# Numbers fetched two steps behind their list, logits in the ring of banks, measuring products at the head of a step

## The chip, the cores and the metric

The kernel runs on one core of a Trainium2 chip. The metric is the device time of one execution in microseconds. The kernel before took 1575.07 us in the median of three runs.

## The reference

A long convolution with a gate, and a mixture of experts with one expert for each token behind it. Shapes: B=4, S=11456, D=128, E=8 experts with F=1024 hidden values.

```python
h_filt = (maximum(pos_emb @ w1, 0) @ w2) * exp(-0.01 * pos)[:, None]
u = x * v
y = irfft(rfft(u, n=2*S) * rfft(h_filt, n=2*S))[:, :S, :]
x = (x * y).reshape(B * S, D)                # the rows of the second half

do_compute = x @ w_skip > 0                  # rows that go through an expert
e_idx = argmax(x[do_compute] @ w_gate)       # its one expert
gate_w = softmax(...)[e_idx]
out = x.copy()
out[do_compute] += gate_w * (maximum(x @ w1[e], 0) @ w2[e])
```

## The kernel before

The program has four parts, one behind the other on each engine: `first_phase` (filter and first transform), `freq_phase` (products in the frequency domain), `out_phase` (last transform, routing and the first expert work) and `late_slots` (the rest of the expert work). The change touches only `out_phase` and the generator `early_slots` that runs inside it.

`out_phase` makes the rows in NCH = 32 chunks of 128 x 12 rows. A chunk `ch` passes through a row of small jobs: `product` (matmuls of the last transform on TensorE, and a multiplication by x on VectorE, L1112, into the tile `xm`), `turned` (transposes), `score` and `score2` (the nine logits of each row, computed turned and then turned back), `choose` (the expert of each row, VectorE), `exp` and `gate`, `count`, `total` and `full` (how many rows each expert gets), `measure` and `ranks` (small matmuls), `measured` and `route` (VectorE), `spread` (one-hot tables on VectorE, in the first FRONT = 7 chunks partly on GpSimd), `collect`, `lay`, `laid`, `write` (the list of row numbers, written to HBM by an indirect DMA of GpSimd, L615).

The order is written by hand. Time is cut into steps; three steps belong to a chunk, so chunk `ch` begins at step `first(ch)` = 0, 4, 7, 10, 13, and on by threes. A table gives each job a lag in steps behind `first(ch)` and an order within its step (a number; jobs of all chunks that fall into one step are sorted by it). So three kinds of step follow each other: those with lags 0, 3, 6, 9, 12 (called step A below), with lags 1, 4, 7, 10 (step B) and with lags 2, 5, 8, 11 (step C). Every instruction is issued in exactly the order that results; an engine never passes an instruction that waits.

Expert work is handed out between the jobs. `next(work)` stands at order 0.5 of each step, and because `PACE` is 1.24 it is called once more at the end of about every fourth step. It issues a piece of `early_slots`: 'up' matmuls (L730 to L732) or 'down' matmuls (L813) of a group of 256 or 512 rows, or the preparation of the next group.

Before an expert can work on rows, these things happen one after the other: the list of a chunk is written (L615, GpSimd's queue); at a few chunks (`KNOWN`) a `table` is computed in five stages that alternate between VectorE and TensorE (L557 to L606; its final stage reads the products of L585 to L587 from PSUM at L590 to L594); `name`, at order 7.5 of each step, fetches the numbers of at most two groups from the list into SBUF (L625, SyncE's queue); one step later the group has its name, and `ex.more()` gathers its rows by two indirect DMAs (L667, GpSimd's queue); and `prepare` splits the weights and transposes the rows (L719). For the first group `prepare` waits a fixed number of steps for the gathered rows.

PSUM: `opy` is a ring of three banks called `wide`, used by `product`, `turned` and `score`. `opl` holds three fixed banks: bank 0 is shared by counting, measuring, ranks and the tables, bank 1 belongs to the down products, bank 2 holds the turned logits `lgp` beside `places` and `lies` (the results of `collect` and `lay`). The dependencies go by bank: who writes a bank waits for all that still read from it.

SyncE's queue carries, in this order of the program, the loads of x (`ox`, L1078) and of the transformed data (`zt`, L1087), the stores of finished chunks (L1116), and the fetches of numbers (L625).

## Time and profile before

| | |
|---|---|
| median of 3 runs | 1575.07 us (1573.11 to 1578.29) |
| the profiled execution, its own time | 1581.42 us |
| its span, first to last instruction | 1579.6 us |
| mean granted clock of TensorE | 0.973 of full speed |
| TensorE busy | 1484.2 us (94% of the span) |
| VectorE busy | 1130.7 us (72%) |
| GpSimd busy | 1080.7 us (68%) |
| ScalarE busy | 755.1 us (48%) |

The profiled execution is 6.35 us longer than the median; 1.8 us of its time lie around the span. Times below are those of this one execution, counted from the span's start. "Idle before" is the time in which an engine had nothing to run, and the arrow names the instruction whose end released it. PEclk is the clock that TensorE was granted: 1.00 is 2.4 GHz and 0.50 is 1.2 GHz.

### The profile page before, as it was taken

The page shows a single profiled execution, that of the slowest core. Times are in us where ns is not written, and L with a number is a line of the kernel's source. Part 1 is how long each engine was busy: PE and PEld are TensorE (multiplying, and loading weights), DVE is VectorE, ACT ScalarE, POOL GpSimd, SP SyncE. Part 2 cuts the span into 40 slices and gives each one's busy share as a digit, 9 for nine tenths or more (in the row PEclk, how much of TensorE's full clock was granted, in tenths as well). Part 3 has the DMA queues.
Part 4 walks back from the last instruction along what each step waited for, and adds up shares of the span by engine and source line. Part 5 has one row for each costly group of instructions (what it writes and reads, how often), then busy time and mean ns, then how long its engine had stood idle before and what let it go on. Part 6 is the DMA issues. An engine that isn't in the chain of part 4 may idle for free. (4 is left out here: it accounts for less than half of the span.)

```text
span 1579.6 us, 24184 instructions
## 1 busy us (share of the span) xinstructions
PE 1484.2 (94%) x7360; PEld 931.2 (59%) x7360; DVE 1130.7 (72%) x2323; ACT 755.1 (48%) x1509; POOL 1080.7 (68%) x832
## 2 busy tenths in 40 slices
PE   8976999999999999998759999999989999999998
PEld 3542444444444444443437767777777888888888
DVE  2324877888788889996757877777766777777774
ACT  5542555544545444442224554444535555555554
POOL 2102988888888878882157566875777888888756
PEclk9996999999999999999789999999989999999999
DMA  9998999999999978978968888988521111111100
GB/s 322 332 337 316 382 372 375 359 331 331 314 353 330 311 237 271 351 202 286 352 193 259 252 276 263 283 282 249 174 63 35 46 46 45 46 46 43 43 25 29
DMA packets 200376, 361.82 MB, mean 229 GB/s; under 512 B 64492, under 2 KB 140762, under 8 KB 200206
## 3 DMA queue, kind: packets, MB, share of 16 engines
q1 hardware_dynamic: 181078, 317.04, 59.5%
q0 software_dynamic: 16448, 38.88, 8.5%
q10 hardware_dynamic: 2720, 4.34, 0.9%
q8 instruction: 59, 0.97, 0.3%
q14 instruction: 71, 0.58, 0.1%
HBM read 216.77 MB, written 145.42 MB: 229 GB/s over the span
## 5 line engine op out<-in xcount | busy, mean ns | idle before, releaser
L412 PE MATMUL ps<-y,c 128*128 128x512 f32 x720 | 331.3, 597 | 0.3
L480 POOL TENSOR_TENSOR y<-y,p 128x2048 f32<-128x2048 f32 x59 | 267.8, 4538 | 70.0 <-DVE p L401 70.0
L736 POOL DMA_INDIRECT out<-o,ids x182 | 199.3, 1095 | 116.3 <-DVE o L743 78.6
L412 PEld LDWEIGHTS ps<-y,c 128*128 128x128 f32 x720 | 133.4, 190 | 173.0 <-issue 156.5
L667 POOL DMA_INDIRECT xt<-out,ids x182 | 192.8, 1059 | 58.4 <-issue 29.1
L401 DVE TENSOR_TENSOR p<-xp,g 128x1024 f32<-128x1024 f32 x240 | 217.4, 948 | 0.0
L401 DVE TENSOR_TENSOR y<-xp,g 128x1536 f32<-128x1536 f32 x120 | 210.9, 1757 | 4.0
L852 DVE SCALAR_TENSOR_TENSOR hh<-hp,hh 128x1024 fp32r<-128x1024 f32 x122 | 148.7, 1219 | 88.9 <-ACT hh L851 75.5
L413 ACT COPY z<-ps 128x512 f32<-128x512 f32 x180 | 105.6, 586 | 178.3 <-PE ps L412 158.6
L851 ACT ACTIVATE hh<-hp 128x1024 fp32r<-128x1024 f32 x122 | 126.4, 1036 | 92.1 <-issue 70.4
L481 POOL TENSOR_TENSOR y<-y,p 128x1024 f32<-128x1024 f32 x59 | 139.1, 2357 | 4.6
L640 POOL MEMSET idle<- 128x512 f16 x231 | 126.3, 547 | 0.3
L381 PE MATMUL xp<-x,wf 128*128 128x480 f32 x256 | 117.4, 583 | 9.1 <-DMA x<-x1f 5.9
L210 PE MATMUL ps<-wf,c 60*120 60x384 f32 x512 | 112.6, 536 | 11.6 <-DVE wf L193 11.6
L212 ACT COPY wf<-ps 120x384 f32<-120x384 f32 x256 | 105.6, 493 | 27.0 <-PE ps L210 23.8
L813 PE MATMUL bank<-wd,h 128*128 128x128 f32 x896 | 114.8, 286 | 0.0
L193 POOL TENSOR_TENSOR wf<-wf 124x768 f32<-124x768 f32 x45 | 82.0, 1822 | 47.5 <-DVE g L394 47.4
L813 PEld LDWEIGHTS bank<-wd,h 128*128 128x128 f32 x896 | 108.0, 198 | 0.3
L730 PE MATMUL hp<-hl,ws 128*128 128x512 f32 (+1 forms) x256 | 103.2, 403 | 2.6 <-issue 1.5
L393 DVE TENSOR_TENSOR g<-xp,g 128x128 f32<-128x128 f32 x120 | 34.8, 290 | 97.2 <-ACT g L386 97.1
L384 ACT COPY g<-xp 64x192 f32<-64x192 f32 x120 | 38.0, 317 | 137.4 <-PE xp L381 94.7
L707 DVE TENSOR_TENSOR ws<-wf,ws 128x1024 fp32r<-128x1024 f32 x82 | 99.9, 1218 | 5.0 <-issue 3.2
(199 smaller groups left out, 2851.3 us busy)
## 6 DMA issues: line engine op xcount, KB each, us to landing
wf<-xv SPq DMA_DIRECT2D x64, 768.0 KB
x1d<-wf SPq DMA_DIRECT2D x64, 720.0 KB
x<-x1d SPq DMA_DIRECT2D x60, 768.0 KB
zt<-zd SPq DMA_DIRECT2D x60, 768.0 KB
zd<-z SPq DMA_DIRECT2D x110, 384.0 KB
out<-xm SPq DMA_DIRECT2D x96, 258.0 KB
ox<-xo SPq DMA_DIRECT2D x96, 256.0 KB
x1f<-fx POOLq DMA_DIRECT2D x16, 720.0 KB
```

The lines of the kernel that those rows point to most:

```text
L210: nc.tensor.matmul(ps[p], self.c1[rows], u[rows, q * RUN:(q + 1) * RUN], start=True, stop=True)
L381: nc.tensor.matmul(xp[:, k, 0:(NS + NB) * DH], c2(n % PER * KS + j * KH + k), x1[:, j * KH + k], start=True, stop=True)
L401: nc.vector.tensor_tensor(o[:, :, :, j * KH:(j + 1) * KH].rearrange("p s a k b d -> p (s a) k b d"), x[:, None].broadcast_to([128, m, KH, ...
L412: nc.tensor.matmul(zps, c3[:, a, :], y[:, blk, a], start=(a == 0), stop=(a == 1))
L480: nc.gpsimd.tensor_tensor(y[:, 1:], y[:, 1:], p1, ALU.add)
L481: nc.gpsimd.tensor_tensor(y[:, 2:], y[:, 2:], p2, ALU.add)
L640: self.nc.gpsimd.memset(self.idle, 0.0)
L667: ins = nc.gpsimd.indirect_dma_start(out=xt[:, j], out_offset=None, in_=self.rows[0:have], in_offset=bass.IndirectOffsetOnAxis(ap=ids[:, j ...
L736: ins = nc.gpsimd.indirect_dma_start(out=self.rows, out_offset=bass.IndirectOffsetOnAxis(ap=ids[:, j:j + 1], axis=0), in_=o, in_offset=Non ...
L813: nc.tensor.matmul(bank[:, j * D:(j + 1) * D], h[f][:, j * 128:(j + 1) * 128], wd[s][:, f * D:(f + 1) * D], start=(f == 0), stop=(f == F / ...
L851: nc.scalar.activation(h[:, 0], hp, AF.Relu)
L852: nc.vector.scalar_tensor_tensor(h[:, 1], hp, 0.0, h[:, 0].bitcast(F32), ALU.max, ALU.subtract)
```

## The change

Six things are done. `STORE` goes from 7 to 6: each store is issued one step sooner. `prepare` waits three steps instead of two for the rows of the first group. `lgp`, the logits turned back, are no longer in bank 2 but in a bank of the ring `wide`, and `score2` moves behind `turned`, from order 2 to 4.2 of its step. `name` fetches the numbers of a list only if the list was written two steps ago, not one. `measure` and `ranks` move from the end of step C (lag 8) to the head of the following step A (lag 9), and with them `measured` and `routed`, which were already there, move behind the first call of `tabled` at order -1.5, so that a table begins and ends one step later. `spread` moves from the head of step C (lag 11) to the middle of the step B before it (lag 10), and the second half of the load of `zt` from lag 1 to the end of lag 0.

```diff
-STORE = 7
+STORE = 6
...
-                for _ in range(4 if s else 2):
+                for _ in range(4 if s else 3):
                     yield
...
-        lgp = bank[2][:, 0:NB * 128].rearrange("p (s t) -> p s t", s=NB)
-        places, lies = bank[2][0:PQ, 384:384 + PL], bank[2][0:PQ, 384 + PL:385 + PL]
+        places, lies = bank[2][0:PQ, 0:PL], bank[2][0:PQ, PL:PL + 1]
...
         def score2(ch):
             lt = chunks.pop(ch)
+            lgp = wide()[:, 0:NB * 128].rearrange("p (s t) -> p s t", s=NB)
...
-                if b not in ex.tabled or written.get(ch, at[0]) >= at[0]:
+                if b not in ex.tabled or written.get(ch, at[0]) >= at[0] - 1:
                     return
...
-                    (0, 0, produced), (1, 0.1, lambda ch: load_z(ch + ZB, 1)), (1, 4, turned),
-                    (3, -0.1, score), (4, 2, score2), (5, 3, choose), (6, 1, exp), (6, 4.5, count), (6, 6, counted), (6, 6, gate), (7, 4.4, total),
-                    (8, -2.5, full), (8, 4.4, measure), (8, 4.5, ranks),
-                    (9, -2.3, measured), (9, -2, routed), (11, -2.4, spread), (12, 0.2, collect), (12, 0.3, lay), (12, 2.5, laid), (12, 2.6, write)):
+                    (0, 0, produced), (0, 8.9, lambda ch: load_z(ch + ZB, 1)), (1, 4, turned),
+                    (3, -0.1, score), (4, 4.2, score2), (5, 3, choose), (6, 1, exp), (6, 4.5, count), (6, 6, counted), (6, 6, gate), (7, 4.4, total),
+                    (8, -2.5, full), (9, -0.4, measure), (9, -0.35, ranks),
+                    (9, -0.3, measured), (9, -0.2, routed), (10, 3, spread), (12, 0.2, collect), (12, 0.3, lay), (12, 2.5, laid), (12, 2.6, write)):
```

Lines 1055 to 1137 of the kernel before have numbers one lower in the changed kernel.

**The first group on TensorE.** The rows L719 are the transposes of the first group's gathered rows; L571 to L587 are the table of the chunk with index 4; L1178 counts the experts of a chunk. Before, TensorE came to L719 in the step B of chunk 7, right behind the first products of that table:

```order
L1178 LDWEIGHTS oh
L1178 MATMUL bank_4478<-ones,oh 96x1
L571 LDWEIGHTS shift
L571 MATMUL bank_4478<-tnt,shift 8x1
L572 LDWEIGHTS shift
L572 MATMUL bank_4478<-done,shift 8x1
L719 MATMUL mh<-ident,xt_4442 128x128 x2
L1140 MATMUL bank_4480<-ident,lt 128x128 x3
L1124 MATMUL wide<-ident,xm 128x128 x12
```

Now L719 stands in the step B of chunk 8, three steps later; the rest of the table, and the measuring, logits, products and collecting of a whole chunk (L1198 to L1213, here from the last rows of the collecting on), are in front of it, and `score2` (L1140) is behind the transposes of `turned` (L1123, before L1124):

```order
L1250 MATMUL bank_4480<-hl,hq 53x32
L1213 MATMUL bank_4480<-ge_4481 53x1
L1178 LDWEIGHTS oh
L1178 MATMUL bank_4478<-ones,oh 96x1
L719 MATMUL mh<-ident,xt_4442 128x128 x2
L1123 MATMUL wide<-ident,xm 128x128 x12
L1140 MATMUL wide<-ident,lt 128x128 x3
```

So the work of three steps moved from behind the first group's transposes to ahead of them.

**The first fetch on SyncE.** L625 is the fetch of a group's numbers (with L623 and a register operation for its address), here of the first two groups. Before, the loads of x and `zt` for the next chunk stood behind it and behind a second pair of fetches:

```order
L1087 DMA zt<-zd 128x4x384
L623 TENSOR_LOAD addr
L623 ISA x2
L625 REGISTER_ALU
L625 DMA ids<-lists 128x2
```

Now one more store stands ahead of the first pair, and loads of the next chunk come right behind it, ahead of the second pair:

```order
L1115 DMA out<-xm 128x516 x2
L623 TENSOR_LOAD addr
L623 ISA x2
L625 REGISTER_ALU
L625 DMA ids<-lists 128x2
L623 TENSOR_LOAD addr
L623 ISA x2
L625 REGISTER_ALU
L625 DMA ids<-lists 128x2
L1115 DMA out<-xm 128x516
L1075 DMA c_5265<-c 128x256
L1077 DMA ox<-xo 128x512 x3
```

The first pair of fetches moved one step towards the end of the program.

**A table and the measuring product on TensorE.** L585 to L587 are the last products of a table (that of the chunk with index 8, with three entries), L1198 is the measuring product; both use bank 0. Before, a piece of expert work (L813, 'down') stood between them:

```order
L586 MATMUL bank_4478<-tpast,tstep 1x3
L587 LDWEIGHTS done
L587 MATMUL bank_4478<-first,done 1x3
L813 MATMUL bank_4479<-wd,h 128x128 x8
L1198 LDWEIGHTS sums
L1198 MATMUL bank_4478<-ct,sums 128x2
```

Now nothing stands between them:

```order
L586 MATMUL bank_4478<-tpast,tstep 1x3
L587 LDWEIGHTS done
L587 MATMUL bank_4478<-first,done 1x3
L1198 LDWEIGHTS sums
L1198 MATMUL bank_4478<-ct,sums 128x2
```

On VectorE the final stage of the same table (L590 to L594) stood behind `full` and `spread` (L1242, L1244). Now it stands behind `choose` (L1149 to L1159), and `measure` waits for its last row:

```order
L582 CAST tph<-tpast 8x3
L1149 TENSOR_REDUCE mx<-lg 128x12
L1151 TENSOR_TENSOR df<-lg,mx 128x96
L1153 SCALAR_TENSOR_TENSOR wt<-df,rev 128x96
L1155 TENSOR_REDUCE mw<-wt 128x12
L1157 SCALAR_TENSOR_TENSOR me<-lg,mw 128x12
L1159 TENSOR_TENSOR oh<-rev,me 128x96
L590 SCALAR_TENSOR_TENSOR trow<-iota,bank_4478 1x3
L593 TENSOR_SCALAR addr<-trow 1x3
L594 TENSOR_SCALAR tab<-bank_4478 1x3
```

The table's last stage moved one step on, to the head of the step in which the measuring product is now.

## Rows read from the trace of the kernel before

**Rows 1.** Busy time by stretch: bounds in us, then for each engine busy us and (instructions), then the granted clock, the DMA share and GB/s. `out_phase` begins at 731.5 us. The first stretch ends with the first group's transposes; in the second, expert work runs beside the jobs of the chunks; the third holds the end of `out_phase`; the last is `late_slots` without its end.

```profile
801.00:816.00 15.00, 1.19 (x5) 0.90 (x6) 4.38 (x16) 1.40 (x3) 9.85 (x11) 0.62 0.62 188
830.00:1140.00 310.00, 297.15 (x2435) 220.18 (x2434) 234.31 (x891) 146.98 (x298) 213.92 (x250) 1.00 0.82 258
1140.00:1196.00 56.00, 50.56 (x353) 42.81 (x352) 32.36 (x135) 19.73 (x33) 43.14 (x51) 0.91 0.26 57
1196.00:1540.00 344.00, 341.41 (x1617) 281.81 (x1618) 256.46 (x371) 200.71 (x234) 265.46 (x276) 1.00 0.16 42
```

**Rows 2.** Timeline of TensorE around the first group's transposes: start us, busy us, the instruction, [idle before it and what ended that].

```profile
800.79 0.16 PE L571 MATMUL bank<-tnt,shift 8*8 8x1 f16 x1 [0.99 <-DVE tnt L565]
...
810.63 0.48 PE L719 MATMUL mh<-ident,xt 128*128 128x128 f32 x1 [9.65 <-DMA xt<-out,ids]
815.29 0.47 PE L719 MATMUL mh<-ident,xt 128*128 128x128 f32 x1 [4.19 <-DMA xt<-out,ids]
...
816.20 2.52 PE L1124 MATMUL wide<-ident,xm 128*128 128x128 f32 x12
...
818.82 0.39 PE L730 MATMUL mh<-hl,ws 128*128 128x256 f32 x1
```

**Rows 3.** Timeline of SyncE's queue at the same place (issues of DMAs; the waits for semaphores are not rows of it).

```profile
793.93 0.42 SPq L1087 DMA_DIRECT2D zt<-zd  x1
802.56 1.46 SPq L625 DMA_DIRECT2D ids<-lists  x2
...
807.72 1.34 SPq L1078 DMA_DIRECT2D ox<-xo  x3
```

**Rows 4.** Timeline of GpSimd at the same place.

```profile
793.18 1.59 POOL L615 DMA_INDIRECT lists<-pl,lies  x1 [7.37 <-DVE sm L1170]
...
805.28 2.12 POOL L667 DMA_INDIRECT xt<-out,ids  x1 [7.72 <-DMA ids<-lists]
...
808.12 1.02 POOL L667 DMA_INDIRECT xt<-out,ids  x1 [0.17 <-issue]
```

**Rows 5.** Busy time by stretch, columns as in rows 1: one chunk without expert work, first as TensorE passes it and then as VectorE does, and the 3 us behind the wait of rows 2.

```profile
792.90:800.80 7.90, 6.24 (x57) 3.69 (x58) 5.94 (x28) 2.58 (x6) 2.96 (x3) 1.00 0.91 288
794.80:803.70 8.90, 4.55 (x42) 1.96 (x41) 8.21 (x36) 2.73 (x6) 1.34 (x2) 1.00 0.66 207
815.00:818.00 3.00, 2.71 (x13) 2.71 (x14) 0.47 (x2) 1.21 (x3) 2.67 (x4) 0.50 1.06 358
```

**Rows 6.** Timeline of VectorE between 777 and 803 us.

```profile
777.12 1.89 DVE L1112 TENSOR_TENSOR xm<-wide,ox 128x512 f32<-128x512 f32 x3 [0.96 <-DMA out<-xm]
...
794.85 0.15 DVE L1191 TENSOR_SCALAR nt<-bank 96x1 int32<-96x1 f32 x1 [1.35 <-PE bank L1186]
...
795.30 0.81 DVE L1242 TENSOR_TENSOR hq<-grid,tf 128x636 f16<-128x636 f16 x1
796.03 0.55 DVE L1242 TENSOR_TENSOR hl<-grid,tf 128x384 f16<-128x384 f16 x1
...
802.87 0.18 DVE L1257 SCALAR_TENSOR_TENSOR pl<-bank,no 53x32 int32<-53x32 f32 x1
```

**Rows 7.** Waits of TensorE between 830 and 1140 us: who waited <- for whom: us in total, times, longest us.

```profile
PE bank L1198 <- DVE tdn L599: 4.5, 3, 1.8
PE bank L1250 <- POOL hl L1244: 2.9, 1, 2.9
...
PE bank L1140 <- DVE pl L1257: 1.4, 2, 1.1
PE bank L1198 <- DVE tab L594: 1.3, 1, 1.3
```

**Rows 8.** Timelines at the table of the chunk with index 8, TensorE first, then VectorE.

```profile
873.24 0.16 PE L587 MATMUL bank<-first,done 8*1 8x3 f16 x1
873.33 2.05 PE L813 MATMUL bank<-wd,h 128*128 128x128 f32 x16
876.69 0.21 PE L1198 MATMUL bank<-ct,sums 96*128 96x2 f16 x3 [1.30 <-DVE tab L594]
...
876.10 0.14 DVE L590 SCALAR_TENSOR_TENSOR trow<-iota,bank 1x3 f32<-1x3 f32 x1
...
876.49 0.14 DVE L594 TENSOR_SCALAR tab<-bank 1x3 int32<-1x3 f32 x1
...
877.36 0.61 DVE L743 SCALAR_TENSOR_TENSOR o<-bank,xt 128x128 f32<-128x128 f32 x2
877.88 0.24 DVE L1149 TENSOR_REDUCE mx<-lg 128x12 f32<-128x96 f32 x1
...
879.24 0.26 DVE L1159 TENSOR_TENSOR oh<-rev,me 128x96 f16<-128x96 f32 x1
```

**Rows 9.** Timeline of ScalarE: the copies of `turned` out of the ring, and the copy of a group's weights.

```profile
794.00 1.56 ACT L1127 COPY xT<-wide 128x512 f32<-128x512 f32 x3 [0.24 <-PE wide L1124]
...
801.92 1.04 ACT L702 CAST ws<-wf 128x1024 fp32r x1 [0.75 <-DVE xm L1112]
```

**Rows 10.** Waits of SyncE's queue between 731 and 1200 us, columns as in rows 7.

```profile
SPq L1078 <- DVE xm L1112: 126.7, 40, 14.1
SPq L625 <- DMA lists<-pl,lies: 43.9, 7, 9.0
```

**Rows 11.** Waits of TensorE between 1140 and 1200 us, the longest one.

```profile
PE bank L1250 <- DVE hl L1244: 1.5, 1, 1.5
```

## The prediction

> **What bounds the kernel now.** I read the page's busy times first, then busy time by stretch, then the waits of TensorE in the stretches that the change touches. From 830 us on TensorE is the bound: it is busy 297.15 of 310 us beside the chunks and 341.41 of 344 us in the late groups, at full clock [rows 1]. Its work is the same in both kernels, so time can only be won or lost where TensorE stands still or runs at the lower clock between 731 and 1196 us, and whatever is won there arrives at the end, because nothing later waits for anything but TensorE.
>
> The largest such place is one hole. Between 801 and 816 us TensorE is busy 1.19 us [rows 1]: it has reached the transposes of the first group and waits 9.65 us for its first 128 rows and 4.19 us for the second 128 [rows 2]. The other four engines show why. The list that holds the group's numbers was issued at 793.18 us [rows 4]. SyncE had issued its last load at 793.93 and did not issue the fetch until 802.56 [rows 3]: it stood still for the list, with a wait of 9.0 us at the longest in this part [rows 10]. The gathers followed at 805.28 and 808.12 [rows 4], and the second landed when TensorE went on, at 815.29 [rows 2].
>
> From 830 to 1140 us TensorE's waits are few and each has a name [rows 7]: 4.5 + 1.3 us at the measuring product for the table's last stage, 2.9 us for a one-hot table that GpSimd multiplies, 1.4 us of the turned logits for a reader of the same bank.
>
> **Part 1: the first group three steps later (fetch one step, gathered rows one step, and one more step through the extra call).** The jobs of a whole chunk now run ahead of the transposes. TensorE's share is 6.24 us busy, read over one such chunk without expert work [rows 5]. Can they run in the hole? They are bound by VectorE: 8.21 us busy of 8.90 for one chunk [rows 5]. So TensorE, which stopped at 801, would reach the transposes at about 801 + 8.9 = 809.9 us. When do the rows land now? The fetch is a step later in the program, but SyncE stood waiting for the list over that step anyway, and its issue stays at 802.56. The first gather passes behind the next list on GpSimd; that list needs VectorE's `pl`, done at 803.05 [rows 6], and takes 1.59 us [rows 4], so it is out of the way by about 804.7, before the 805.28 of the old gather. So the rows land at 815.3 as before, and TensorE still waits some 5.4 us, but it has done 6.24 us of work that stood behind the wait. That is the lower value, 6.2 us. The upper one: `spread` (0.81 + 0.55 us) now fills a time in which VectorE waited 1.35 us for `total` [rows 6] in each chunk, and two such chunks stand between the table and the list; the list, and all behind it, would come 1.35 to 2.7 us sooner, and the loads at 807.72 [rows 3], which now stand ahead of the second fetch, are out of the way sooner too. I allow 3.5 us at most, 9.7 in all, and take 7.7, nearer to the lower value, since the list's landing hangs on other transfers.
>
> The clock: behind the hole it stands at 0.50 [rows 5], and the twelve transposes take 2.52 us [rows 2], against TensorE's work at the full clock. 2.71 us of work in that stretch would be about half of it at full clock, so 1.4 us, and 1.9 us with the transposes before it, can be won if the shorter wait keeps the clock up; nothing if not. I take 1.0.
>
> **Part 2: table one step later, at the head of step A.** In the front its first product no longer waits for VectorE right behind `route` (0.99 us [rows 2]); VectorE bounds that stretch, so I count 0.5, between 0 and 1.0. In the part where TensorE is the bound there are four tables (indices 8, 13, 22, 28). They cost 5.8 us today [rows 7]. The cover was a piece of expert work of 2.05 us between the table's products and the measuring product [rows 8]. For the tables of 8 and 22 nothing stands there now, and `choose` stands on VectorE ahead of the last stage. `choose` is 877.88 to 879.50, 1.6 us, the last stage 876.10 to 876.63, 0.5 us [rows 8]; VectorE can start on `choose` only when it has handed over what the products read, so the wait is about 1.6 + 0.5 = 2.1 us each. For those of 13 and 28 a 'down' piece still stands there, but its result is taken off by VectorE ahead of the last stage: 0.61 us for two rows of them [rows 8], twice that for the larger group, plus 0.5 and a release: 1.3 and 1.9 us. Sum 7.4, 1.6 more than today; the products L585 may also wait for VectorE now, a few tenths each. I take a loss of 2.5. The bounds are 0, and 7 if VectorE comes a whole `choose` late at each (4 x 1.6). Behind the waiting product stand `score` and `product`; VectorE waits for these, not the other way round.
>
> **Part 3: logits in the ring.** The 1.4 us for a reader of bank 2 [rows 7] go. In their place `score2` waits for the first copy of `turned` out of the ring. A copy takes 1.56 / 3 = 0.52 us [rows 9], and TensorE has two more blocks of transposes to do meanwhile, so it is hidden unless ScalarE is behind. That is so in the two chunks (16 and 24) where a weight copy of 1.04 us [rows 9] stands just ahead of it: at most 2 x (1.04 + 0.52) = 3.1 us; I take 0.5.
>
> **Part 4: `spread` a step sooner, stores a step sooner, the second `zt` load at the end of its step.** `spread` a step sooner gives GpSimd a step more: the 2.9 us [rows 7] should go; bounds 0 and 2.9. The stores: the 0.96 us that VectorE waited for one [rows 6] lies where part 1 counts VectorE. SyncE now waits at the first store for `gate` of the same step; behind it stand only the next steps' stores, fetches and the loads of x, and those wait for VectorE's products anyway, 126.7 us in all [rows 10]. The `zt` load is now ahead of the store and may be behind two fetches; it is read two chunks later, 17.8 us even without expert work, so a wait of 9.0 us [rows 10] is hidden.
>
> **The end of `out_phase`** (50.56 of 56 us busy, with the clock at 0.91 [rows 1]): table and `spread` of the last chunk shift by a step against the expert pieces. The longest wait, 1.5 us for `spread` [rows 11], can go or another like it can come. I count 0, between -3 and +3.
>
> **Sum.** -7.7 - 1.0 - 0.5 + 2.5 - 1.4 + 0.5 - 2.9 + 0 = -10.5 us. Against the profiled execution's 1581.42 us that is 1570.9; the median of the runs is 6.35 us lower, so I predict 1575.07 - 10.5 = 1564.6 us.
>
> The DMA page of the Trainium skill ("DMA: Bandwidth & Descriptors", section on the anatomy of a DMA by the gpsimd path) gives a transfer of this kind about 2 us of fixed cost. By that the list would have landed near 797 us, SyncE would have had no wait to hide the later fetch in, and the gain would be that of the first rival below. The trace disagrees: 793.18 to 802.56 us.
>
> **Rivals.** *The hole moves with the group.* If the first fetch, which is a step later, makes the rows land a step later (8.9 / 3 = 3.0 us), part 1 gives 6.2 - 3.0 = 3.2 us, no clock is won, and what parts 2 to 4 give (1.3) is lost to the end of the phase: 1571.9 us. For it speaks that GpSimd and SyncE are in strict order; against it, the wait of 9 us ahead of the fetch.
>
> *More.* All upper values: 9.7 + 1.9 + 1.0 + 1.4 + 2.9, no loss at the tables or in the ring, 3 at the end: 1555 us. It needs everything at once, the tables above all.
>
> *Slower: the measuring product behind the table.* One place, the wait L1198 at the head of step A. Without part 2 the sum is -13.0; it turns into slower if the four tables cost more than 5.8 + 13.0 = 18.8 us, 4.7 each. VectorE would have to come 4 us late into step A: it carries, in B and C, the taking off of a group, `spread`, `full`, the table and `choose`. At 6 us each (24) the time is 1575.1 + 5.2 = 1580.3. Against it: VectorE is busy 234 of 310 us [rows 1], and the longest such wait now is 1.8 us [rows 7].
>
> *Slower through the ring.* If `score2` waited a whole copy in each of 32 chunks, 32 x 0.52 = 16.6 us would be lost, against a sum of -11.0 without the ring's own loss: 1580.7. Today nothing of this ring shows among the longest waits of TensorE [rows 7]. The Trainium skill ("TensorE: Matmul & The Clock Gate", section on the second failure mode, cycling of the PSUM queue) warns that cycling through banks makes TensorE idle a little so often that its clock falls back. By that the lower clock would come on top; the trace shows the ring turning seven times a chunk at a granted clock of 1.00.
>
> **Chances and range.** The forecast 0.48 (1558 to 1569), the hole that moves 0.26 (1569 to 1576), more 0.13, the tables 0.09, the ring 0.04. A change below 0.3% (4.7 us) can't be told from none, so faster means below 1570.3. All of the forecast and of 'more' and somewhat over half of the first rival lie there: 0.76. Of the rest of that rival and the two last, 0.15 stays within 0.3% and 0.09 is slower. The range 1555 to 1574 leaves out the two slower cases and the edges.
>
> **What would show it.** Right: L719's wait for the gathered rows below 7 us in all, with the products of chunk 8 ahead of it; L1198 behind L594 at 1.5 to 3 us in the tables of 8 and 22; no wait of L1140 for L1257, of L1250 for GpSimd; SyncE's wait for lists shorter. Wrong: rows landing after 818 us, waits of L1198 above 4 us, waits of L1140 for L1127 in many chunks, or the clock at 0.50 for long behind the last chunk.

## The result, and the profile after

The changed kernel takes 1590.26 us in the median of 8 runs, the kernel before 1577.97 in 8 runs beside it: ratio 1.008, with a 95% interval of 1.0061 to 1.0099 (one disturbed execution, of 6247 us, is left out). So the change is slower by some 12 us, where 10.5 us less was forecast and a range of 1555 to 1574 us. The profiled execution took 1588.61 us, with a span of 1586.8.

Busy time by stretch, columns as in [rows 1]; the first, second and fourth row answer to rows there:

```profile
801.00:816.00 15.00, 8.72 (x64) 4.14 (x62) 10.93 (x46) 3.33 (x9) 13.35 (x17) 0.77 0.98 296
830.00:1140.00 310.00, 291.00 (x2324) 211.41 (x2326) 223.21 (x846) 137.23 (x284) 203.79 (x239) 0.98 0.80 246
860.00:870.00 10.00, 6.16 (x29) 1.86 (x29) 6.82 (x36) 2.08 (x4) 1.99 (x3) 0.66 0.22 69
1140.00:1196.00 56.00, 49.93 (x372) 40.67 (x372) 31.67 (x141) 23.01 (x40) 43.68 (x54) 0.94 0.27 59
```

Most of the hole is filled: 8.72 us busy of 15, against 1.19. But beside the chunks, where TensorE was busy 297.15 of 310 us at a clock of 1.00, it is now busy 291.00 at 0.98, and one stretch of 10 us stands out with 6.16 busy and a clock of 0.66.

TensorE at the first group's transposes, which answers to [rows 2], and then SyncE and GpSimd ([rows 3, 4]):

```profile
801.20 0.16 PE L571 MATMUL bank<-tnt,shift 8*8 8x1 f16 x1
...
803.92 0.16 PE L585 MATMUL bank<-tph,onesf 8*1 8x4 f16 x1 [2.54 <-DVE mx L1149]
...
806.65 0.22 PE L1198 MATMUL bank<-ct,sums 96*128 96x2 f16 x3 [2.49 <-DVE tab L594]
...
808.42 4.19 PE L1110 MATMUL wide<-zt,c 128*64 128x512 f32 x12
...
813.01 0.42 PE L719 MATMUL mh<-ident,xt 128*128 128x128 f32 x2
```

```profile
797.95 1.46 SPq L625 DMA_DIRECT2D ids<-lists  x2
...
789.98 1.59 POOL L615 DMA_INDIRECT lists<-pl,lies  x1 [10.10 <-DVE sm L1170]
...
802.24 1.06 POOL L667 DMA_INDIRECT xt<-out,ids  x1 [0.17 <-issue]
...
804.02 1.07 POOL L667 DMA_INDIRECT xt<-out,ids  x1 [0.17 <-DVE mx L1149]
```

L719 doesn't wait at all. The list is 3.2 us sooner than before, the rows are there, and what holds TensorE here now is the table: 2.54 us ahead of its last products, 2.49 ahead of the measuring product, and 4.19 us for a product that takes 2.79 at full clock.

Waits of TensorE between 830 and 1140 us, columns as in [rows 7]:

```profile
PE bank L1198 <- DVE tdn L599: 7.0, 3, 2.9
PE wide L1140 <- ACT xT L1126: 2.6, 4, 0.8
PE bank L585 <- DVE mx L1149: 2.6, 1, 2.6
PE bank L1198 <- DVE ct L1193: 2.5, 3, 1.2
PE bank L1198 <- DVE tab L594: 1.6, 1, 1.6
...
PE bank L585 <- DVE tph L582: 0.8, 1, 0.8
```

The waits of L1250 for GpSimd and of L1140 for L1257 are gone, as forecast. The tables (L585, and L1198 for L599 and L594) hold TensorE for 12.0 us, against 4.5 + 1.3 = 5.8 in [rows 7]. The table of chunk 8 shows how, TensorE first and then VectorE, beside [rows 8]:

```profile
857.83 0.16 PE L571 MATMUL bank<-tnt,shift 8*8 8x1 f16 x1
...
859.37 0.28 PE L732 MATMUL mh<-hl,ws 128*128 128x256 f32 x1
862.23 0.16 PE L585 MATMUL bank<-tph,onesf 8*1 8x3 f16 x1 [2.59 <-DVE mx L1149]
...
864.08 0.22 PE L1198 MATMUL bank<-ct,sums 96*128 96x2 f16 x3 [1.61 <-DVE tab L594]
...
864.41 1.51 PE L1132 MATMUL wide<-xT,wg 128*32 128x384 f32 x8
865.85 4.49 PE L1110 MATMUL wide<-zt,c 128*64 128x512 f32 x12
```

```profile
857.64 0.14 DVE L569 CAST tnt<-tni 8x1 f16<-8x1 int32 x1
...
858.25 0.81 DVE L1242 TENSOR_TENSOR hq<-grid,tf 128x636 f16<-128x636 f16 x1
...
859.56 0.56 DVE L1244 TENSOR_TENSOR hl<-hl,val 128x384 f16<-128x384 f16 x1
...
860.80 0.81 DVE L581 TENSOR_SCALAR tpast<-iota,tcum 8x3 f32<-8x3 f32 x1
861.64 0.54 DVE L582 CAST tph<-tpast 8x3 f16<-8x3 f32 x1
861.72 0.46 DVE L1149 TENSOR_REDUCE mx<-lg 128x12 f32<-128x96 f32 x1
...
863.88 0.14 DVE L594 TENSOR_SCALAR tab<-bank 1x3 int32<-1x3 f32 x1
```

Between the table's first stage (L569) and its middle one (L581, L582) now stand two rows of down results, the whole of `spread` (1.9 us from 858.25) and `full`; between the middle and the last (L594) stands `choose`. On TensorE 1.7 us of 'up' matmuls stand in the first gap and nothing in the second. So TensorE waits twice, 4.2 us in all, and its next products run in part at the lower of its two clocks, 1.2 GHz (the mean from 860 to 870 us is 0.66): L1132 takes 1.51 us instead of 0.85, L1110 4.49 instead of 2.79, another 2.4 us.

To compare kernels I use two lengths read from the timelines: the *way*, from TensorE's first row in `out_phase` (L1110, or L1111 before) to its first row of `late_slots`, and the *end*, from TensorE's last row to the end of the span. Between them lie the late groups, 379 to 380 us in every profile of these two kernels. The way was 461.4 us before (731.51 to 1192.86) and 465.7 after (731.39 to 1197.12); the end 6.50 and 9.84. Together +7.7. The rest of the 12 us isn't in this pair of profiles: the profiled execution of before took 1581.42 us, longer than any of the eight runs, that of the changed kernel 1588.61, below its median.

### The profile page after: what moved, and what is told of

Read it like the earlier page. It is cut to its first block, busy times and chain, and to the rows that moved or that the text cites. A ratio compares the mean times of both kernels' runs of the same rounds, so it can differ in the third digit from the quotient of the medians.

```text
span 1586.8 us, 24174 instructions
## 1 busy us (share of the span) xinstructions
PE 1490.2 (94%) x7360; PEld 925.6 (58%) x7360; DVE 1130.9 (71%) x2323; ACT 751.5 (47%) x1509; POOL 1074.7 (68%) x832
## 5 line engine op out<-in xcount | busy, mean ns | idle before, releaser
L667 POOL DMA_INDIRECT xt<-out,ids x182 | 189.5, 1041 | 40.7 <-issue 28.4
L210 PE MATMUL ps<-wf,c 60*120 60x384 f32 x512 | 113.4, 537 | 12.5 <-DVE wf L193 12.4
L615 POOL DMA_INDIRECT lists<-pl,lies x32 | 52.3, 1636 | 90.6 <-DVE sm L1170 53.6
L813 PE MATMUL bank<-wd,h 128*128 128x128 f32 x896 | 110.5, 279 | 0.0
L1110 PE MATMUL wide<-zt,c 128*64 128x512 f32 x384 | 102.9, 660 | 7.3 <-DMA zt<-zd 6.2
L813 PEld LDWEIGHTS bank<-wd,h 128*128 128x128 f32 x896 | 103.7, 192 | 0.7 <-issue 0.2
```

The costliest lines, as they stand in the source:

```text
L210: nc.tensor.matmul(ps[p], self.c1[rows], u[rows, q * RUN:(q + 1) * RUN], start=True, stop=True)
L667: ins = nc.gpsimd.indirect_dma_start(out=xt[:, j], out_offset=None, in_=self.rows[0:have], in_offset=bass.IndirectOffsetOnAxis(ap=ids[:, j ...
L813: nc.tensor.matmul(bank[:, j * D:(j + 1) * D], h[f][:, j * 128:(j + 1) * 128], wd[s][:, f * D:(f + 1) * D], start=(f == 0), stop=(f == F / ...
```

## Experiments

Each is timed against the kernel before in the same session; in the first four and the last three, that kernel itself took 1591 to 1593 us, and the late groups took 391 to 400 us in every kernel profiled there. The way doesn't depend on it, as the repeated kernels show. The table's ways and ends are those of one profiled execution each, the ratios those of all runs.

| kernel | way, us | end, us | ratio to before (95%) |
|---|---|---|---|
| before, again | 460.3 | 6.5 | 0.9985 (0.9963 to 1.0006) |
| changed, again | 467.1 | 9.8 | 1.0076 (1.0051 to 1.0101) |
| changed, measuring back | 452.0 | 9.8 | 0.9994 (0.997 to 1.0018) |
| the same, repeated | 452.4 | 9.8 | 0.9967 (0.9953 to 0.998) |
| before + group later alone | 456.1 | 9.8 | 1.0029 (1.0006 to 1.0052) |
| the same, repeated | 455.6 | 9.8 | 1.0004 (0.9983 to 1.0024) |
| before + measuring move alone | 466.5 | 6.5 | 1.0069 (1.004 to 1.0098) |
| before + part 4 alone | 443.1 | 6.5 | 0.9912 (0.9877 to 0.9947) |
| changed, group back | 464.0 | 6.5 | 1.0036 (1.0019 to 1.0053) |
| changed, ring back | 464.1 | 9.8 | 1.0032 (1.0006 to 1.0058) |
| changed, tables sooner | 446.7 | 9.8 | 0.997 (0.9951 to 0.9989) |
| the same, repeated | 448.3 | 9.8 | 0.995 (0.993 to 0.997) |
| tables sooner, fetch half only | 444.0 | 9.7 | 0.9943 (0.9926 to 0.9961) |
| tables sooner, prepare half only | 450.5 | 6.6 | 0.996 (0.994 to 0.9981) |
| tables sooner, ring back | 438.8 | 9.8 | 0.9915 (0.9896 to 0.9934) |
| the same, and fetch half only | 437.3 | 9.7 | 0.9917 (0.9891 to 0.9943) |
| changed + one product twice | 466.4 | 9.8 | 1.0071 (1.0045 to 1.0098) |
| before + three small GpSimd memsets | 457.4 | 6.5 | 1.0008 (0.9986 to 1.0029) |

The last two only pad a program (see *The end*), and their times are those of the kernels that they pad. So the changed kernel has ways of 465.7, 466.4 and 467.1 us, and the kernel before 461.4, 460.3 and 457.4: a difference of less than 4 us isn't read from single ways.

**The measuring products.** First taken back out of the changed kernel, then made alone (only the entries that move are shown):

```diff
-(9, -0.4, measure), (9, -0.35, ranks), (9, -0.3, measured), (9, -0.2, routed)
+(8, 4.4, measure), (8, 4.5, ranks), (9, -2.3, measured), (9, -2, routed)
```

> The changed kernel with the measuring products, `ranks`, `measured` and `route` back at the places they had before; everything else stays changed. Theory A (the move of the measuring products is what costs): by it every table starts a step later on VectorE, behind `spread`, and its last stage meets the next measuring product with no TensorE work between. In the trace of the changed kernel the four tables between 830 and 1140 us hold TensorE for 2.59 + 1.61 + 2.87 + 0.81 + 2.38 + 1.79 = 12.05 us against 5.85 before, and the granted clock falls to 0.66, 0.88 and 0.83 behind three of them, which I put at some 5.8 us of longer products: 12 us in all. So this kernel should be at about 1590 - 12 = 1578 us or, with the waits for `full` gone too, 1575; the waits of L1198 and L585 should be as before, and the clock 1.00 from 830 to 1140. Theory B (the hole's gain is given back in any case, because the groups' chain or the leftover expert work is late, and the tables only show it): 1586 to 1591 us.

> The same kernel as the first experiment (measuring products back, all else changed), on another chip. On the chip of the first four experiments the late groups took 391 to 400 us in every kernel, where the kernel before, the changed one and two more take 379 to 380 us elsewhere. Theory A: the out phase up to the late groups takes 452 us as there (461 in the kernel before, 466 in the changed one), the late groups 380, the end 9.84: about 5 us faster than the kernel before, 0.996 to 0.998. Theory G (the late groups are slow because the group was moved, not because of that chip): 391 us or more for the late groups, no gain.

> The kernel before with only the measuring products, `ranks`, `measured` and `route` moved to the head of the next step. Theory A: the tables' waits and the lower clock behind them come with this edit alone: 10 to 14 us slower than the kernel before, ratio 1.006 to 1.009, with L585 waiting over 2 us in the table of chunk 8 and the clock below 0.9 behind it. Theory B: 0 to 3 us slower.

The way without the move is 452.0 and 452.4 us, 14 us less than with it (465.7 and 467.1), and the time is 0.3% below the kernel before in the session without long late groups. From 830 to 1140 us its trace reads

```profile
830.00:1140.00 310.00, 297.84 (x2422) 219.91 (x2422) 231.36 (x893) 145.30 (x300) 213.75 (x253) 1.00 0.79 251
```

which is the busy time and the clock of before [rows 1]; the tables hold TensorE there for 1.5 us instead of 12.0. Over the whole way, with the move and without it (columns as in [rows 1], of the engines TensorE alone):

```profile
731.39:1197.12 465.73, 419.36 (x3240) 0.96 0.76 237
```

```profile
732.39:1184.79 452.40, 416.71 (x3240) 0.97 0.77 244
```

TensorE is idle 46.4 us with the move and 35.7 without it, and the same products take 2.7 us longer with it; in the other pair of profiles the two differences are 10.1 and 5.0 us. The first of the two runs fell on a chip where every kernel is longer, so its 1588 us says nothing; its ratio of 0.9994 does, since theory A's 1575 to 1578 us are 0.998 to 1.000 of the kernel before and theory B's 1586 to 1591 are 1.005 to 1.008. Made alone, the move lengthens the way by 5.6 us (9 against the padded kernel before) and the time by 0.7%, 11 us (6 to 16), with the same kinds of wait (L585 2.5 + 2.3 us, L1198 4.1); in the table of chunk 8 L585 waits 1.2 us, not the 2 expected, and the clock behind it is 0.83. Theory A holds, theories B and G fall. Whether the move costs more beside the other edits than alone is not shown.

**The tables' place.** Is it the measuring product at the head, or the table that now starts behind `spread`? The table's first call in a step is put right behind `route` (again only the entry that moves):

```diff
-(-1.5, tabled, (0,))
+(-0.15, tabled, (0,))
```

> The changed kernel with the first of the two places in a step at which a table's next stage is written moved from ahead of the measuring products to right behind `route` of the same step (order -1.5 to -0.15). A table then starts in the step of its `route`, ahead of `spread` on VectorE, its last stage stands a step ahead of the next measuring product, and the measuring products stay at the head of the step. Theory A (the table's place against `spread` and the measuring product is the cause): L1198 no longer waits for the last stage, L585 no longer for a stage behind `spread`, the clock stays at 1.00, 12 to 16 us faster than the changed kernel: 1574 to 1578 us, and if the hole's gain then stays, below the kernel before. Theory C (the measuring product at the head is itself late, behind `full`, whatever the table does): L1198 waits for `full` (L1193) and little is won, 1584 to 1590 us.

> The same kernel as the fourth experiment (the changed kernel with the tables' stage right behind `route`), on another chip. Theory A: 447 us up to the late groups, 380 for them, 9.84 at the end: 10 us faster than the kernel before, 0.993 to 0.995. Theory G: 391 us for the late groups, the same as the kernel before.

19 us off the way, 0.3 to 0.5% below the kernel before, with the measuring products still at the head. The table of chunk 8 on TensorE in the repeated run:

```profile
852.22 0.16 PE L571 MATMUL bank<-tnt,shift 8*8 8x1 f16 x1
...
852.34 3.84 PE L813 MATMUL bank<-wd,h 128*128 128x128 f32 x32
...
857.82 0.16 PE L585 MATMUL bank<-tph,onesf 8*1 8x3 f16 x1
...
860.68 0.21 PE L1198 MATMUL bank<-ct,sums 96*128 96x2 f16 x3 [1.00 <-DVE addr L593]
...
860.94 0.85 PE L1132 MATMUL wide<-xT,wg 128*32 128x384 f32 x8
861.72 2.79 PE L1110 MATMUL wide<-zt,c 128*64 128x512 f32 x12
```

L585 has 5.5 us of cover and doesn't wait, L1198 waits 1.00, L1110 runs at full clock. From 830 to 1140 us the tables hold TensorE for 1.6 us instead of 12.0, and the clock is 1.00. So the place of the table against `spread` and `choose` is the cause. Theory C falls: the wait of the measuring products for `full` (L1193) that it named is there, 2.5 us, but it is the same 2.5 us in the changed kernel.

**The group.** Made alone, taken back, and in halves, the fetch half (first pair of lines) and the prepare half (second pair), these beside the tables' new place:

```diff
-if b not in ex.tabled or written.get(ch, at[0]) >= at[0]:
+if b not in ex.tabled or written.get(ch, at[0]) >= at[0] - 1:
-for _ in range(4 if s else 2):
+for _ in range(4 if s else 3):
```

> The kernel before with only the numbers fetched a step later and the first group prepared a step later. Theory A: the hole at 801 to 816 us is filled as in the changed kernel (TensorE busy about 8.7 of 15 us instead of 1.2) and nothing is given back: 6 to 9 us faster than the kernel before, ratio 0.994 to 0.996. Theory B: the hole closes but the same time comes back as leftover expert work behind the chunks or as waits of the later groups: within 2 us of the kernel before.

> The same kernel as the second experiment (before with the numbers a step later and the group prepared a step later), on another chip. Theory A: 456 us up to the late groups, 380 for them, 9.84 at the end: 456 + 380 + 9.84 against 461 + 380 + 6.5, about 1.5 us faster than the kernel before, 0.998 to 1.000. Theory G: 395 us or more for the late groups, slower by 10 us.

> The changed kernel with the numbers fetched one step behind their list and the first group prepared two steps behind it, as before; all else stays changed. If the later group is worth what it was taken for, this kernel is 6 to 8 us slower than the changed one up to the last product of TensorE, with the hole back at about 801 to 816 us. At its end it should be 3.3 us shorter: of six profiles, the two without this edit have 6.50 us between TensorE's last product and the end of the span, the four with it 9.82 to 9.84. Together 3 to 5 us slower than the changed kernel, ratio to before 1.010 to 1.012. If the later group is worth nothing, it is 3 us faster than the changed kernel, ratio 1.005 to 1.007.

> The fourth experiment's kernel (tables right behind `route`) with the first group prepared two steps behind its gathers again; the numbers are still fetched two steps behind their list. Up to the late groups: 3 us later than with both halves (451 instead of 448 us), since TensorE reaches the first transposes a step sooner and waits that step for the rows. At the end: 9.84 us behind the last product if the later fetch (lists ahead of gathers in GpSimd's queue) lengthens GpSimd's drain, 6.5 if the later group does. Ratio to before 0.997 with 9.84, 0.995 with 6.5.

> The fourth experiment's kernel with the numbers fetched one step behind their list again; the first group is still prepared three steps behind its gathers. Up to the late groups: the transposes come a step sooner in the program than with both halves; if SyncE's wait for the list hides the later fetch, as I took it, the rows land at the same time and TensorE waits 3 us more (451 us). At the end: 6.5 us if the later fetch is what lengthens GpSimd's drain. Ratio to before 0.995 with 6.5, 0.997 with 9.84.

Alone the edit fills the hole (TensorE busy 8.64 us of 15) and shortens the way by 5 us against the first two profiles of the kernel before, by 1.5 against the third, where 6 to 9 were expected; the end is 3.3 us longer. No gain can be measured (1.0029 and 1.0004). In the changed kernel it doesn't shorten the way at all: without it the way is 464.0 and the ratio 1.0036, below both ranges expected. The expectation of 451 us for the fetch half was a miss: with it alone L719 waits only 2.0 us, and the way is 3.5 us shorter than with both. Beside the fetch half, the step more for `prepare` leaves more work behind the last measuring product: TensorE is busy 35.1 us there with both halves, 31.6 with the fetch half, 31.3 in the kernel before. The prepare half alone leaves the hole open (L719 waits 8.6 us); its way and its end are as expected.

The hole is not equally large in every execution of one kernel. In the kernel before run again L719 waits 8.6 us where it waited 9.65 + 4.19 in [rows 2]:

```profile
808.99 0.48 PE L719 MATMUL mh<-ident,xt 128*128 128x128 f32 x1 [5.58 <-DMA xt<-out,ids]
...
812.44 0.48 PE L719 MATMUL mh<-ident,xt 128*128 128x128 f32 x1 [2.97 <-DMA xt<-out,ids]
```

In the padded kernel before it waits 8.8 us, and 7.6 to 10.1 in the other kernels that fetch the numbers as early as before.

**The end.** Every kernel with the fetch half has 9.7 to 9.8 us behind TensorE's last product, every other one 6.5 to 6.6. Two steps of GpSimd's queue make the difference, its drain (L1448; the three figures are shortest/median/longest in ns) and a step on its DMA semaphore (L992); before, then after:

```profile
L1448 POOLq DRAIN  x3: 46/103/1214, 1577.6 to 1579.3; - x3
...
L992 POOLq INC_SWDGE_SEM  x1: 488/488/488, 1575.7 to 1575.7; - x1
```

```profile
L1448 POOLq DRAIN  x3: 46/103/3909, 1582.1 to 1586.5; - x3
...
L992 POOLq INC_SWDGE_SEM  x1: 1142/1142/1142, 1579.5 to 1579.5; - x1
```

(3.91 - 1.21) + (1.14 - 0.49) = 3.35 us. Two paddings asked whether the length of a program decides, TensorE's (in `measure` of the changed kernel) or GpSimd's (in `space` of the kernel before):

```diff
-for k in range(3):
+for k in (0, 1, 2, 2) if ch == 0 else (0, 1, 2):
...
+for _ in range(3):
+    nc.gpsimd.memset(self.idle[:, 0:1], 0.0)
```

> The changed kernel with one measuring product of the first chunk given twice, so that TensorE's program is two instructions longer, as long as before (15285 instead of 15283); all other engines' programs stay as they are. Theory E (the 3.3 us at the end hang on where the end of TensorE's program lies, not on anything that the change schedules): 6.5 us behind the last product instead of 9.84, 3 us faster than the changed kernel, ratio to before 1.004 to 1.006. Theory F (they hang on the last stores, the lists or the other engines' programs): 9.84 us, no difference from the changed kernel.

> The kernel before with three tiny GpSimd memsets (128 x 1) at the start of the out phase, nothing else. GpSimd's program is then 2207 instructions long, where kernels with 6.5 us behind TensorE's last product have 2202 or 2203 and those with 9.84 have 2206. In the traces the 3.3 us are two steps of GpSimd's own end: its drain takes 3.91 us instead of 1.21 and a step on its DMA semaphore 1.14 instead of 0.49. Theory H (the place at which GpSimd's program ends decides): 9.8 us behind the last product, 3 us slower than the kernel before, ratio 1.001 to 1.003. Theory F (what GpSimd's transfers have done before decides, or their order): 6.5 us, ratio 0.999 to 1.001.

Neither: an end of 9.8 us with the first, a drain of 1.21 us and an end of 6.5 with the second. E and H fall, and the halves tried apart show that it is the fetch half. What it changes for GpSimd is the order of its transfers, since the later fetch puts lists ahead of gathers in its queue, hundreds of microseconds before the end. That the order does it is inferred from this, not isolated, and why it should lengthen the drain is open.

**The ring.** Logits back in bank 2 and `score2` back at order 2, once beside the tables' new place and once in the changed kernel:

> The fourth experiment's kernel with the logits turned back in bank 2 and `score2` at its old place. By my sum the ring wins 1.4 - 0.5 = 0.9 us, so this kernel would be 1 us slower, ratio 0.995 to 0.997. By the waits in the trace (2.9 us of L1140 for the copies of `turned` and 1.3 us of it in the front, against 1.4 + 0.5 us and 2.8 in the front for a reader of bank 2 in the kernel before) the ring is worth between -1 and +1 us, and `choose`, with more time behind `score2`, is the only thing that can tell: 0.994 to 0.997.

> The changed kernel with the logits turned back in bank 2 and `score2` at its old place; all else stays changed. If the ring costs in the changed kernel what it cost beside the tables' new place (448 against 439 us up to the late groups), this kernel is 5 to 9 us faster than the changed one: ratio to before 1.002 to 1.005. By the sum of the prediction it is 1 us slower: 1.008 to 1.010.

Without the ring the way is 8 to 9.5 us shorter beside the tables' new place and about 2 us shorter in the changed kernel. By the runs it is 5 to 9 us there (0.9915 against 0.997 and 0.995) and 7 us here (1.0032 against 1.008 and 1.0076, inside the first range expected). So the ring is a cost, not the gain of 0.9. The first 100 us of the way, with the ring and without it (columns as in [rows 1], the second row busy time of TensorE alone):

```profile
733.11:833.11 100.00, 81.14 (x562) 45.43 (x563) 73.13 (x272) 32.28 (x76) 34.78 (x38) 0.90 0.94 317
```

```profile
728.36:828.36 100.00, 80.36 (x593) 0.94 0.98 327
```

31 matmuls more in the same time, with the clock at 0.94 instead of 0.90. Over the whole way the idle time differs by 2.5 us (the waits of L1140 for the copies go, those for L1257 come back) and the busy time for the same instructions by 7. In the changed kernel the first 100 us have 0.90 and 0.85 with the ring (two profiles) and 0.93 without. But with the fetch half alone they have 0.91 with the ring and 0.92 without, though the way differs by 6.7 us, and the kernel before, which has no logits in the ring, has 0.85, 0.83 and 0.86. That the ring costs is shown; that its waits pull the clock down is argued from the first pair and not shown.

**Part 4 alone.** `spread`, the stores and the second load of `zt`, in the kernel before:

> The kernel before with `spread` a step sooner, the stores a step sooner and the second load of `zt` at the end of its step, nothing else. By the sum: 2.9 us faster (0.997 to 0.999), no wait of L1250 for GpSimd. By difference (the changed kernel without the measuring products is 4 us better up to the late groups than the group's part alone, and the ring in it may cost 5 to 9): 9 to 13 us faster, 0.992 to 0.994.

The way is 17 us shorter (14 against the padded kernel before), the time 0.9% or 14 us less, the best of the edits made alone and more than either forecast. By the measuring product of chunk 3, before the hole, 4.6 to 7.6 us are won against the three profiles of the kernel before. TensorE at the fifth product of the way, before (run again) and with this edit:

```profile
762.97 0.48 PE L1250 MATMUL bank<-hl,hq 128*53 128x32 f16 x12 [1.68 <-DVE ct L1193]
...
767.57 5.39 PE L1111 MATMUL wide<-zt,c 128*64 128x512 f32 x12 [2.97 <-issue]
```

```profile
759.07 0.48 PE L1250 MATMUL bank<-hl,hq 128*53 128x32 f16 x12 [0.60 <-DVE sm L1171]
...
761.63 2.79 PE L1111 MATMUL wide<-zt,c 128*64 128x512 f32 x12 [0.76 <-issue]
```

`collect` (L1250) waits 1.1 us less for VectorE, and the product runs at full clock, where it takes 5.39 us here and 4.17 and 5.39 in the other two profiles of the kernel before. Its wait ahead (for nothing that the profile shows) is 1.4 and 1.5 us in those, so most of the 2.2 us by which it is shorter here is no effect of the edit. By the measuring product of chunk 8 the lead is 5 to 12 us, from that of chunk 14 on 8 to 16. Which of its three edits wins how much was not taken apart.

**Together.** Tables sooner, ring back, fetch half only:

> The changed kernel with the tables right behind `route`, the logits in bank 2 and the first group prepared two steps behind its gathers. If what the two undone parts won adds up (439 us up to the late groups with the ring back, 4 us less with the group prepared sooner), 435 + 380 + 9.8 us: 13 to 17 us faster than the kernel before, 0.989 to 0.992. If both won the same wait, 0.991 to 0.993 as with the ring back alone.

The shortest way, 437.3 us, and 0.9917 of the kernel before, as good as the ring back alone (0.9915) and part 4 alone (0.9912); the intervals don't tell the three apart. All beat both kernels. The kernels of before and after were also run again for the comparison:

> The kernel before, unchanged, profiled once more on the chip of the next three runs, so that stages can be compared on one chip. Between TensorE's first product of the out phase and its first product of the late groups I expect 461 us, as in the profile before, from there to its last product 380 us if the chip doesn't matter and about 391 if the late stage of the first four experiments (391 to 400 us in each) was the chip's, and 6.5 us behind the last product.

> The changed kernel, unchanged, on the same chip. 0.6 to 1.0 per cent slower than the kernel before; 465 us from the first product of the out phase to the first of the late groups, and 9.84 us behind TensorE's last product, as in its first profile.

Of all kernels run twice unaltered, way and end repeat within 1.6 us; the padded kernel before shows that they can differ by 4.

## Why the prediction was wrong

The step that failed is part 2, the tables. Its reading of the order was right: nothing stands between the last products and the measuring product, `choose` stands ahead of the last stage. The waits of L1198 that it added up from this, 7.4 us, came out near that: 1.61 + 2.87 + 2.38 + 1.79 = 8.65 us. But it followed only this last gap. The gap before it, between the table's first and last products, was passed over with "a few tenths each": there `spread` and `full` now stand on VectorE, and L585 waits 2.59 us in chunk 8 and 0.81 in chunk 22, and 2.58 and 2.54 in the two tables of the front, where 0.5 was booked as a gain for L571. And no clock was counted behind the waits, though one was counted behind the hole; it made 2.4 of the 6.6 us of chunk 8's table. Booked: +2.5 - 0.5 = 2.0. Measured by undoing it: 14 on the way, 13 to 18 by the runs; on the way 10 to 11 us of it are waits and 3 to 5 longer products. The rival *Slower: the measuring product behind the table* named this place, but at 4.7 us a table and with L1198 alone, and gave it 0.09; its argument against it, VectorE's mean busy share, says nothing about four single places.

All the signs that were to show the prediction right are there: L719 doesn't wait, L1198 waits 1.6 and 2.4 us in the tables of 8 and 22, the waits for L1257 and of L1250 for GpSimd are gone, and SyncE's waits for lists between 731 and 1200 us fell from 43.9 to 21.8 us. None of them looks at L585, so all could come true in a kernel that is slower.

Without part 2 the sum was -12.5 us, and the way without it is 8.6 us shorter (5 against the padded kernel before). That this is as near as it is, is luck, for its terms were off both ways:

- **Part 1** (-7.7, and -1.0 for the clock): the hole closed as described, and the list came 3.2 us sooner, more than the 1.35 to 2.7 allowed. Alone it won 1.5 to 5 us. First, the hole of 9.65 + 4.19 us in the profile that was read is the largest of all; the next two profiles of that kernel have 8.6 and 8.8. Second, TensorE's work is the same, but what a later group doesn't do in the hole it does later: with the edit alone TensorE is busy 35.0 us behind the last measuring product, 3.7 more than before, and the end of the phase was counted at 0 without following it.
- **Part 3** (-1.4 + 0.5): the waits for L1257 went, but waits for the copies came, 2.6 us beside the chunks and 1.3 in the front, and, beside the tables' new place, 7 us more of busy time for the same products. Undone, this part gives back 2 us of the way in the changed kernel (7 us by the runs) and 8 to 9.5 beside the tables' new place. The Trainium skill ("TensorE: Matmul & The Clock Gate", section on the second failure mode) warns of small idle times in a cycle of PSUM banks that pull the clock down. Of two pairs of profiles one agrees in the front, 0.90 with the ring and 0.94 without, and the other hardly, 0.91 and 0.92. The rival on the ring had the direction right; its price, a whole copy in each chunk, was too high.
- **Part 4** (-2.9): 14 to 17 us. The term counted one wait of L1250 and left what `spread` does in the front to part 1. Over the whole way TensorE is idle 8 to 12 us less than in the three profiles of the kernel before and busy 6 to 9 us less for the same products. VectorE's waits for `total`, which part 1 had seen, explain little of it: they are 1.9 us in all between 731 and 800 us, in two chunks. What else makes up the gain is open.
- **The end of the program**: 3.35 us that no step of the prediction had. It held that whatever is won arrives at the end, and looked for no effect of the fetch behind the last product.

As sums of the way: 460.8 before (mean of the first two profiles), less 8.6, plus 14.2 for the tables, is 466.4 after; with 3.3 at the end that makes +8.9 us of the 12 that the runs show. The remaining 3 lie in which executions were profiled: the first two of before were 3 us longer than the medians of that kernel (1581.42 against 1577.97, 1580.31 against 1576.99), the two of after 2 to 3 us shorter (1588.61 against 1590.26, 1588.21 against 1590.98). The padded kernel before, profiled in an execution of median length, has a way of 457.4, and with that the sum is 9.0 + 3.3 = 12.3 us.

Three smaller slips of the prediction change nothing: the upper bound at the tables is 4 x 1.6 = 6.4, not 7; what parts 2 to 4 give is 1.8 by the sum, not 1.3; and over half of the first rival was put below 1570.3 us, though its own value is 1571.9.

## What to carry to other kernels

A chain that alternates between two engines is as long as what stands between its stages on both: when it is moved, read every gap on either engine, not only the last one, and add what the products behind each wait lose at the lower clock. Where one edit wins and another loses, undo each alone: here what part 4 won was hidden by what the tables and the ring cost. Read the hole that a change is to close in more than one execution of the kernel: the one priced here was 13.8 us in one profile and 8.6 and 8.8 in the next two. A group of edits that looks like bookkeeping, part 4, can be worth more than the one that closes the largest hole.

## What the runs showed of the hardware

The drain of GpSimd at the end takes 1.21 to 1.30 us in the seven profiles without the later fetch and 3.83 to 3.91 in the thirteen with it, the same in both profiles of a kernel, with 182 gathers and 182 stores in all of them. It goes with the fetch; the order of the transfers is the likely reason, not a shown one.

A small VectorE operation can last as long as what GpSimd does at the time. In the table above L581 ends at 861.61 and L582 at 862.18; GpSimd's rows there are

```profile
860.64 0.98 POOL L736 DMA_INDIRECT out<-o,ids  x1 [0.17 <-issue]
861.62 0.54 POOL L640 MEMSET idle<- 128x512 f16 x1
```

and end at 861.62 and 862.16. Where GpSimd does nothing, the same two take 0.21 and 0.16 us instead of 0.81 and 0.54 (856.99 and 857.24 in the repeated run with the tables sooner). Over all twenty profiles the 26 rows of L581 with no GpSimd row beside them take 0.21 us (one 0.30), the 145 with one beside them 0.21 to 1.39. So the table's middle stage, 1.38 us here and 0.41 there, is stretched by 1.0 us of the 2.59 that L585 waits, by an engine off the critical path.
